# Row sums from a column of ones in the values, norm weights multiplied in on GpSimd: a local-attention and feed-forward kernel on one core

## Chip, cores and metric

The kernel runs on one NeuronCore of a Trainium2 chip. The metric is the device time of one execution in microseconds; lower is better. TensorE is called PE below, VectorE DVE, ScalarE ACT, GpSimd POOL, and SyncE, which only issues transfers here, SP.

## What is computed

Attention over 2 x 8 heads of 768 positions and 64 dimensions, in which every query sees the 31 keys around it and, for each of the 24 blocks of 32 positions, the maximum of the block's keys and the mean of its values. Its output is 1536 tokens of 512 features. They go through a root-mean-square norm with weights and a gated feed-forward layer (1536 wide), and then through a second feed-forward layer (2048 wide) with a squared rectifier. All in float32.

```python
k_sum = k.reshape(B, H, nb, block, D).max(axis=3)
v_sum = v.reshape(B, H, nb, block, D).mean(axis=3)
scores_l = np.where(mask_l, scale * np.matmul(q, k.transpose(0, 1, 3, 2)), -1e9)
scores_s = scale * np.einsum('bhsd,bhnd->bhsn', q, k_sum) + np.log(block)
scores_all = np.concatenate([scores_l, scores_s], axis=-1)
a = np.exp(scores_all - np.max(scores_all, axis=-1, keepdims=True))
a = a / (np.sum(a, axis=-1, keepdims=True) + 1e-09)
x = np.matmul(a, np.concatenate([v, v_sum], axis=2))        # -> tokens x 512
rms = np.sqrt(np.mean(x * x, axis=-1, keepdims=True) + 1e-06)
xn = x / rms * rms_g
x = (silu(xn @ w_gate) * (xn @ w_val)) @ w_out
r = np.maximum(x @ w_in, 0.0)
out = (s * (r * r) + b) @ w_out2
```

## The kernel before

**Tiles and stages.** The 1536 tokens are 12 blocks of 128 (i from 0 to 11; blocks 0 to 5 are batch 0). The attention of a block is done in two units of four heads (g = 0, 1), so there are 24 units. A unit is:

- `do_qk` (L580): four matmuls give scores of 128 queries by 120 columns (96 keys of a window of 64 queries, 24 block summaries) in a PSUM bank. The two halves of 64 queries have windows of their own; queries with zeros in the other half's rows make one matmul serve both.
- `do_top` (L590), per head on DVE: adds the mask, scales, and accumulates the extreme of the row into the tile `sm`. Each is two instructions, the second of which (128x1) writes out the accumulator.
- `do_exp` (L597), per head on ACT: exponential in place; `accum_out` also gives the row sum, in a second instruction that reads the accumulator.
- `do_t` (L608), four transposes of the probabilities P on PE, and `do_pt` (L627), their copy from PSUM to SBUF on ACT.
- `do_rc` (L614, L615) on POOL: 1e-9 is added to the four row sums and they are raised to the power -1.
- `do_pv` (L637): eight matmuls of 64 columns with the values, for four heads and two halves.
- `do_norm` (L644) on DVE: the result in PSUM times the reciprocals, into one half of the block's tile `xn`.

After the second unit of a block: `do_rms` (L663, sum of squares on ACT), `do_ss` (L668, L669, mean and power -0.5 on POOL), the multiplication by this root and by the weights `gbc` in place on DVE (L671), `do_e` (L679, four transposes on PE) and `two_x` (L692, L694: a rounded high part on ACT and the rest on DVE, as matmul operands). A matmul with float32 accuracy is then made of three passes: high by high (L779), low part of the weights by high (L780), high by low (L783), 12 matmuls in all.

**Values.** `load_v` (L297) brings, for two windows at a time, 96 rows of 8 x 64 values into a slot of `vst`; rows 96 to 119 are the block means, made on PE (`add_v` L340, `mean_v` L347), put into the first slots by ACT and DVE in turn (`put_v`, L356 and L354) and spread to the others by transfers from SBUF to SBUF (`spread_v`, L359).

**Weights.** Weight strips arrive as 64-bit floats and are made into float32 by one instruction on ACT (L224) and three on DVE (L233, L234, L235), then split into a high part on ACT (L246) and a low part on POOL (L250). Nine strips are prepared during the attention stage.

**What sets the order.** The attention stage is not written in a loop. `plan` makes a list of tasks, each with an engine, an estimated duration, what it depends on, a rank, and buffers that it takes and gives back; `give_out` runs through a model of time, lets each engine take the ready task of lowest rank, and issues the instructions in that order. Each engine then executes its own list strictly in order. Where the model sees PE idle for over 0.6 us it puts in four transposes of the identity (L461), which compute nothing. For the first three of twelve column strips of the gated layer the matmuls (`mm`, 18 groups of 12) are tasks too: six groups need the blocks 0 to 3, six the blocks 4 to 7, six the blocks 8 to 11. They stand between the attention units in PE's order. Behind the plan, the rest of the two layers is written as plain loops (`moe`).

SP issues every transfer in order; an entry waits for the transfer eight places ahead of it, and a query load (L491) also for the matmuls that last read its buffer.

Of the kernel before, what the change touches and what calls it, by code (L numbers as in the profile page):

```python
# [21 lines left out]
NTL = SEQ // 128  # L22
# [3 lines left out]
HQ = 64  # L26
KW = HQ + 2 * WIN
# [5 lines left out]
NT = NB * NTL  # L33
SUB = 512
# [9 lines left out]
RCENG = "POOL"  # L44
# [6 lines left out]
GENG = "DVE"  # L51
# [6 lines left out]
def kernel(ctx: ExitStack, tc: tile.TileContext, q_t, k_t, v_w, w_gate, w_val, w_out, w_in2, w_out2, rms_g, s2, b2, out):  # L58
# [11 lines left out]
    xnp = pool("xn", 2)  # L70
    rawp = pool("raw", 3)
# [34 lines left out]
    mone = const.tile([128, NH], F32, name="mone")  # L106
# [9 lines left out]
    part = const.tile([128, NSUB * 4 * SUB], F32, name="part")  # L116

    def big():
        return hgp.tile([128, NSUB * 2 * SUB], F32, tag="hg", name="hg")

# [4 lines left out]
    store = [big() for _ in range(5)] + [part[:, i * 3072:(i + 1) * 3072] for i in range(2)]  # L125
# [4 lines left out]
    vst = [[t.rearrange("p (s c) -> p s c", s=NTL) for t in ts] for ts in ((store[1], store[2]), (store[5], store[6]))]  # L130
# [4 lines left out]
    def consts_ident():  # L135
        make_identity(nc, ident)
        nc.gpsimd.memset(mhalf, -0.5)
        nc.gpsimd.memset(mone, -1.0)
# [194 lines left out]
    def add_v(b, a, i):  # L333
# [3 lines left out]
        for s in range(4 * a, 4 * a + 4):  # L337
            j = s % 4
            n0 = 12 * (s % 2) + s // 2
            nc.tensor.matmul(mean_ps[b][32 * j:32 * j + 32], sel[0:64, 17 - n0:49 - n0], vslot(b, s)[0:64], start=a == 0, stop=a == 2)  # L340
# [8 lines left out]
    def put_v(b, s, eng):  # L349
        p0 = 64 if s % 2 else KW  # L350
        o = vslot(b, s)[KW:KC]
        a = mean_ps[b][p0:p0 + NS]
# [5 lines left out]
    def spread_v(b, s):  # L358
        nc.sync.dma_start(out=vslot(b, s)[KW:KC], in_=vslot(b, s % 2)[KW:KC])  # L359
# [3 lines left out]
    rings = {"raw": 3, "wa": 3, "wh": 6, "wl": 6, "xn": 2, "sm": 3, "ks": KSB, **RINGS}  # L363
# [112 lines left out]
    def plan(x):  # L476
# [6 lines left out]
        K, Q, V, KM, VM = {}, {}, {}, {}, {}  # L483
# [16 lines left out]
        def lv(b, t, rank):  # L500
            V[b, t] = task("SP", mb(96 * 4096), lambda: load_v(b, 2 * t, 2), rank=rank)
# [37 lines left out]
        def means(b, rank):  # L539
# [13 lines left out]
            for t in range(NTL):  # L553
# [4 lines left out]
                else:  # L558
                    VM[b, t, "ok"] = [task("SP", 0.3, lambda s=s: spread_v(b, s), puts, 2 * (6 * b + t) - 6) for s in (2 * t, 2 * t + 1)]
# [4 lines left out]
        X_of = {}  # L564
# [4 lines left out]
        for n, (i, g) in enumerate(us):  # L569
# [24 lines left out]
            def do_exp(j, i=i, g=g):  # L594
# [3 lines left out]
                                     bias=sm_of[i][:, 0, h:h + 1], accum_out=sm_of[i][:, 1, h:h + 1])  # L598
# [4 lines left out]
            ex = [task("ACT", 0.38, lambda j=j, f=do_exp: f(j), [tops[j]], n + 0.5 + j * 0.01) for j in range(GH)]  # L603
# [7 lines left out]
            def do_rc(i=i, g=g):  # L611
                rc = sm_of[i][:, 1, GH * g:GH * g + GH]
# [385 lines left out]
```

## Time and profile before

| | |
|---|---|
| median of 3 runs | 650.69 us (650.45 to 652.07) |
| the profiled execution | 650.68 us, span 648.9 us |
| PE busy | 630.3 us (97% of the span) |
| DVE busy | 373.3 us (58%) |
| ACT busy | 267.4 us (41%) |
| POOL busy | 156.4 us (24%) |
| granted TensorE clock | 0.999 |

The span is from the first to the last instruction of the profiled execution; the time is what the device reports for it. Busy times overlap, since each engine runs its own list. PE's share says that little else can be won at the end of the program than PE's own work; the shares of the other engines are means over a first stage, in which all of them are needed, and a long second one that is mostly matmuls.

### The profile page before, as it was taken

To read this page: it belongs to the slowest core of one execution; us is meant where nothing else is said; L and a number is where in the kernel's file an instruction comes from. 1 tells how busy PE (TensorE), PEld (TensorE's weight loads), DVE (VectorE), ACT (ScalarE), POOL (GpSimd) and SP (SyncE) were. 2 spreads that over 40 slices of the span, in tenths; PEclk is the share of its full clock that TensorE was granted. 3 is DMA by queue.
4 is the path that set the end of the run, shared out by engine and by line. 5 is a ranking of instruction groups with operands and counts; after the bars stand their busy time and mean duration, and the time that the engine had idled before them with its cause. 6 is when DMAs were issued, how large, how long until landed. Compare 5 with 4: busy or idle time off the path is not lost.

```text
span 648.9 us, 8741 instructions
## 1 busy us (share of the span) xinstructions
PE 630.3 (97%) x3260; PEld 518.3 (80%) x3260; DVE 373.3 (58%) x743; ACT 267.4 (41%) x606; POOL 156.4 (24%) x201
## 2 busy tenths in 40 slices
PE   4989989999999999999999999999999999999997
PEld 2676878888888888888888888888888888888886
DVE  3498874225861555644556667870388548845532
ACT  3689894233453333311333335542454045404400
POOL 5368773332221111111111111100221022102100
PEclk9999999999999999999999999999999999999999
DMA  8979530003330111211111111121111211110022
GB/s 269 327 210 315 191 125 2 1 0 98 103 137 21 65 66 65 66 65 66 65 66 66 65 66 65 66 92 39 44 55 66 97 62 42 66 59 2 1 97 97
DMA packets 19778, 56.23 MB, mean 87 GB/s; under 512 B 2536, under 2 KB 2792, under 8 KB 19736
## 3 DMA queue, kind: packets, MB, share of 16 engines
q1 hardware_dynamic: 19736, 55.68, 25.9%
q8 instruction: 25, 0.41, 0.3%
q14 instruction: 17, 0.14, 0.1%
HBM read 51.64 MB, written 3.15 MB: 84 GB/s over the span
## 4 chain that ended last, share of the span: by engine, by line
PE 90%; ACT 4%; DMA 3%; DVE 1%; issue 1%; POOL 0%; SPq 0%; ACTq 0%; DVEq 0%; POOLq 0%
PE b L783 22%; PE b L779 21%; PE b L780 21%; PE b L903 7%; PE b L905 7%; PE b L902 7%; ACT P L597 2%; PE b L580 1%; DMA qz<-in_q_t_dram 1%; PE b L637 1%; PE b L608 1%; DMA hg<-in_k_t_dram 1%; PE b L340 1%; DMA raw<-in_w_val_dram 1%; PE b L679 1%
## 5 line engine op out<-in xcount | busy, mean ns | idle before, releaser
L250 POOL TENSOR_TENSOR wl<-wa,wh 128x512 fp32r<-128x512 f32 x68 | 89.8, 1327 | 387.2 <-ACT wh L246 314.3
L779 PE MATMUL b<-x,wh 128*128 128x512 f32 x288 | 113.4, 394 | 0.0
L780 PE MATMUL b<-x,wl 128*128 128x512 f32 x288 | 112.3, 390 | 0.0
L246 ACT ACTIVATE wh<-wa 128x512 fp32r<-128x512 f32 x68 | 41.5, 626 | 95.3 <-PE b L905 45.5
L783 PE MATMUL b<-x,wh 128*128 128x512 f32 x288 | 77.7, 392 | 0.0
L903 PE MATMUL b<-wl,hg 128*128 128x512 f32 (+1 forms) x196 | 75.2, 385 | 0.0
L902 PE MATMUL b<-wh,hg 128*128 128x512 f32 (+1 forms) x196 | 75.2, 385 | 0.0
L780 PE MATMUL b<-y,wl 128*128 128x512 f32 x192 | 74.8, 390 | 0.0
L779 PE MATMUL b<-y,wh 128*128 128x512 f32 x192 | 74.8, 390 | 0.0
L884 DVE SCALAR_TENSOR_TENSOR b<-u,sbc 128x512 f32<-128x512 f32 x48 | 50.7, 1056 | 35.6 <-ACT u L883 35.6
L779 PEld LDWEIGHTS b<-x,wh 128*128 128x128 f32 x288 | 54.1, 188 | 11.1
L780 PEld LDWEIGHTS b<-x,wl 128*128 128x128 f32 x288 | 54.1, 188 | 10.8
L783 PEld LDWEIGHTS b<-x,wh 128*128 128x128 f32 x288 | 53.6, 188 | 10.9
L780 PE MATMUL b<-hg,wl 128*128 128x512 f32 x144 | 56.1, 390 | 0.0
L779 PE MATMUL b<-hg,wh 128*128 128x512 f32 x144 | 56.1, 390 | 0.0
L804 DVE SCALAR_TENSOR_TENSOR hg<-b,bbc,hg 128x512 fp32r<-128x512 f32 x48 | 36.0, 749 | 28.2 <-ACT hg L803 28.2
L905 PE MATMUL b<-wh,hg 128*128 128x512 f32 (+1 forms) x196 | 51.6, 385 | 0.0
L783 PE MATMUL b<-y,wh 128*128 128x512 f32 x192 | 51.3, 390 | 0.0
L235 DVE SCALAR_TENSOR_TENSOR wa<-raw,wa 128x512 int32<-128x512 int32 x68 | 50.0, 735 | 2.0
L803 ACT ACTIVATE hg<-b,bbc 128x512 fp32r<-128x512 f32 x48 | 33.0, 687 | 42.8 <-DVE b L884 42.8
L234 DVE SCALAR_TENSOR_TENSOR wa<-raw,wa 128x512 int32<-128x512 int32 x68 | 48.7, 717 | 2.0
L911 DVE TENSOR_TENSOR part<-b,part 128x512 f32<-128x512 f32 (+1 forms) x37 | 24.4, 673 | 43.4 <-PE b L905 43.4
(99 smaller groups left out, 970.1 us busy)
## 6 DMA issues: line engine op xcount, KB each, us to landing
raw<-in_w_out_dram SPq DMA_DIRECT2D x28, 512.0 KB
raw<-in_w_in_dram SPq DMA_DIRECT2D x16, 512.0 KB
qz<-in_q_t_dram SPq DMA_DIRECT2D x24, 256.0 KB
raw<-in_w_gate_dram SPq DMA_DIRECT2D x12, 512.0 KB
raw<-in_w_val_dram SPq DMA_DIRECT2D x12, 512.0 KB
hg<-in_k_t_dram SPq DMA_DIRECT2D x5, 576.0 KB
out_dram<-part SPq DMA_DIRECT2D x11, 256.0 KB
hg<-in_v_w_dram SPq DMA_DIRECT2D x6, 384.0 KB
```

Source lines behind the costliest of these rows:

```text
L234: lambda: nc.vector.scalar_tensor_tensor(out=ai, in0=hi, scalar=-0x80000000, in1=ai, op0=ALU.bitwise_and, op1=ALU.bitwise_or),
L235: lambda: nc.vector.scalar_tensor_tensor(out=ai, in0=lo, scalar=29, in1=ai, op0=ALU.logical_shift_right, op1=ALU.bitwise_or),
L246: nc.scalar.activation(out=r(h), in_=a_t[i], func=AF.Copy)
L250: nc.gpsimd.tensor_tensor(out=r(lo), in0=a_t.pop(i), in1=high[i], op=ALU.subtract)
L779: nc.tensor.matmul(ps, r(hi[:, kk * 128:(kk + 1) * 128]), xh, start=kk == 0, stop=False)
L780: nc.tensor.matmul(ps, r(lo[:, kk * 128:(kk + 1) * 128]), xh, start=False, stop=False)
L783: nc.tensor.matmul(ps, r(hi[:, kk * 128:(kk + 1) * 128]), r(act(kk, 1)), start=False, stop=kk == 3)
L804: nc.vector.scalar_tensor_tensor(out=r(dst[1]), in0=ps, scalar=bias, in1=dst[0], op0=ALU.add, op1=ALU.subtract)
L884: after(0, lambda u=u, ps=ps: nc.vector.scalar_tensor_tensor(out=ps, in0=u, scalar=sbc[:, 0:1], in1=u, op0=ALU.mult, op1=ALU.mult))
L902: nc.tensor.matmul(acc, gh, r(ws[e][0][:, cs]), start=e == 0, stop=False)
L903: nc.tensor.matmul(acc, gh, r(ws[e][1][:, cs]), start=False, stop=False)
L905: nc.tensor.matmul(acc, r(ge[e][:, 1]), r(ws[e][0][:, cs]), start=False, stop=e == 3)
```

## The change

1. The values get two more columns per head (VH = 66): they arrive as zeros from the host's layout, and a new task `ones_v` on POOL sets them to 1.0, after each load and before the product. The product of the probabilities with such a column is the row sum, so the exponential no longer accumulates one. The loads, slots and spreads are 528 instead of 512 words per window; `part` and the `hg` tiles grow with them.
2. The two instructions for the reciprocal leave POOL. On DVE, `do_norm` now reads the four sums from PSUM, adds 1e-9, takes the reciprocal and then multiplies.
3. The weights are multiplied in on POOL, from `xn` into a new tile `xg` (two buffers), as a task `do_g` that depends on the normalised block alone. DVE then multiplies `xg` by the root, one number per row, in place (`do_gs`). The buffer of `xn` is given back after this, and no longer after the transposes.
4. The planner's estimates follow: exponential 0.38 to 0.29, normalisation 0.34 to 0.65, weights on POOL 1.35, root on DVE 0.5.

The core of the diff:

```diff
 def load_v(b, s0, n):
     t = vst[b][s0 // NTL][0:KW, s0 % NTL:s0 % NTL + n]
-    nc.sync.dma_start(out=t, in_=v_w[b, :, s0:s0 + n])
+    nc.sync.dma_start(out=t.rearrange("p s h d -> p s (h d)"), in_=v_w[b, :, s0:s0 + n])
+
+def ones_v(b, s0, n):
+    rows = KC if s0 < (4 if b == 0 else 2) else KW
+    nc.gpsimd.memset(vst[b][s0 // NTL][0:rows, s0 % NTL:s0 % NTL + n, :, HD:VH], 1.0)
...
 def lv(b, t, rank):
-    V[b, t] = task("SP", mb(96 * 4096), lambda: load_v(b, 2 * t, 2), rank=rank)
+    V[b, t] = task("SP", mb(96 * 16 * VH * 4), lambda: load_v(b, 2 * t, 2), rank=rank)
+    O[b, t] = task("POOL", 0.12, lambda: ones_v(b, 2 * t, 2), [V[b, t]], rank=rank)
...
     nc.scalar.activation(out=P[:, j], in_=P[:, j], func=AF.Exp, scale=-1.0,
-                         bias=sm_of[i][:, 0, h:h + 1], accum_out=sm_of[i][:, 1, h:h + 1])
+                         bias=sm_of[i][:, 0, h:h + 1])
...
-def do_rc(i=i, g=g):
-    rc = sm_of[i][:, 1, GH * g:GH * g + GH]
-    if RCENG == "POOL":
-        nc.gpsimd.tensor_scalar(out=rc, in0=rc, scalar1=1e-9, scalar2=None, op0=ALU.add)
-        nc.gpsimd.tensor_tensor(out=rc, in0=rc, in1=mone[:, 0:GH], op=ALU.pow)
...
-            nc.tensor.matmul(X[64 * c:64 * c + 64, j * HD:(j + 1) * HD], PT[0:KC, j * 128 + 64 * c:j * 128 + 64 * c + 64],
-                             vv[:, c, h * HD:(h + 1) * HD], start=True, stop=True)
+            nc.tensor.matmul(X[64 * c:64 * c + 64, j * VH:(j + 1) * VH], PT[0:KC, j * 128 + 64 * c:j * 128 + 64 * c + 64],
+                             vv[:, c, h], start=True, stop=True)
...
 def do_norm(i=i, g=g):
+    xv = box["X", i, g][:, 0:GH * VH].rearrange("p (h d) -> p h d", h=GH)
+    rc = sm_of[i][:, 1, GH * g:GH * g + GH].rearrange("p (h o) -> p h o", o=1)
+    nc.vector.tensor_scalar(out=rc, in0=xv[:, :, HD:HD + 1], scalar1=1e-9, scalar2=None, op0=ALU.add)
+    nc.vector.reciprocal(rc, rc)
     nc.vector.tensor_tensor(out=X_of[i][:, g * GH * HD:(g + 1) * GH * HD].rearrange("p (h d) -> p h d", h=GH),
-                            in0=box["X", i, g][:, 0:GH * HD].rearrange("p (h d) -> p h d", h=GH),
-                            in1=sm_of[i][:, 1, GH * g:GH * g + GH].rearrange("p (h o) -> p h o", o=1).broadcast_to([128, GH, HD]),
+                            in0=xv[:, :, 0:HD],
+                            in1=rc.broadcast_to([128, GH, HD]),
                             op=ALU.mult)
-N = [task("DVE", dve(256), do_norm, [C, rc], n + 0.0, free=(C,))]
+N = [task("DVE", 0.65, do_norm, [C], n + 0.0, free=(C,))]
...
-G = task(GENG, dve(512) * 1.2 if GENG == "DVE" else pl(512), lambda i=i: (nc.vector if GENG == "DVE" else nc.gpsimd).scalar_tensor_tensor(
-    out=X_of[i], in0=X_of[i], scalar=box["ss", i][:, 1:2], in1=gbc, op0=ALU.mult, op1=ALU.mult), [S, sml], n - 1)
+def do_g(i=i):
+    XG_of[i] = xgp.tile([128, DM], F32, tag="xg", name="xg")
+    nc.gpsimd.tensor_tensor(out=XG_of[i], in0=X_of[i], in1=gbc, op=ALU.mult)
+
+def do_gs(i=i):
+    nc.vector.tensor_scalar(out=XG_of[i], in0=XG_of[i], scalar1=box["ss", i][:, 1:2], scalar2=None, op0=ALU.mult)
+G0 = task("POOL", 1.35, do_g, [*N, sml], n - 1.5, take=("xg",))
+G = task("DVE", 0.5, do_gs, [S, G0], n - 1, give=(("xn", box["N0", i]),))
```

**What moves.** DVE at the first three normalisations (the names `b_...` are PSUM banks: 395, 417 and 435 hold the first three units' results before, 400, 422 and 439 now). Before:

```order
L644 TENSOR_TENSOR xn<-b_395,sm 128x256
L590 ISA P,sm<-b_407,mask_97 128x120
L590 ISA sm 128x1
L234 SCALAR_TENSOR_TENSOR wa<-raw,wa 128x512
L644 TENSOR_TENSOR xn<-b_417,sm 128x256
...
L235 SCALAR_TENSOR_TENSOR wa<-raw,wa 128x512
L644 TENSOR_TENSOR xn<-b_435,sm 128x256
```

Now:

```order
L641 TENSOR_SCALAR sm<-b_400 128x4
L642 RECIPROCAL sm<-sm 128x4
L643 TENSOR_TENSOR xn<-b_400,sm 128x256
L594 ISA P,sm<-b_410,mask_99 128x120
L594 ISA sm 128x1
L234 SCALAR_TENSOR_TENSOR wa<-raw,wa 128x512
L641 TENSOR_SCALAR sm<-b_422 128x4
L642 RECIPROCAL sm<-sm 128x4
L643 TENSOR_TENSOR xn<-b_422,sm 128x256
L641 TENSOR_SCALAR sm<-b_439 128x4
```

Every normalisation is now three instructions, each of which needs the one before it; the rest of the sequence keeps its order.

POOL in the second half of the attention stage, with the numbers of the buffers behind the names. Before:

```order
L668 TENSOR_SCALAR ss_1304<-ss_1304 128x1
L669 TENSOR_TENSOR ss_1304<-ss_1304,mhalf_95 128x1
L614 TENSOR_SCALAR sm_1164<-sm_1164 128x4
L615 TENSOR_TENSOR sm_1164<-sm_1164,mone_94 128x4
...
L668 TENSOR_SCALAR ss_1379<-ss_1379 128x1
L669 TENSOR_TENSOR ss_1379<-ss_1379,mhalf_95 128x1
L614 TENSOR_SCALAR sm_1334<-sm_1334 128x4
L615 TENSOR_TENSOR sm_1334<-sm_1334,mone_94 128x4
L668 TENSOR_SCALAR ss_1429<-ss_1429 128x1
L669 TENSOR_TENSOR ss_1429<-ss_1429,mhalf_95 128x1
```

Now:

```order
L672 TENSOR_TENSOR xg_1218<-xn_1160,gbc_101 128x512
L667 TENSOR_SCALAR ss_1220<-ss_1220 128x1
L668 TENSOR_TENSOR ss_1220<-ss_1220,mhalf_97 128x1
L672 TENSOR_TENSOR xg_1281<-xn_1209,gbc_101 128x512
L667 TENSOR_SCALAR ss_1284<-ss_1284 128x1
L668 TENSOR_TENSOR ss_1284<-ss_1284,mhalf_97 128x1
```

The product of a block stands ahead of the block's root on the same engine; only for the first and second block does it stand behind it.

SP, the loads behind the spreads of the second batch's means. Before:

```order
L359 DMA part<-part 24x512 x6
L491 DMA qz_104<-in_q_t_dram 128x512
L359 DMA part<-part 24x512 x4
L491 DMA qz_103<-in_q_t_dram 128x512
L218 DMA raw<-in_w_val_dram 128x1024
```

Now:

```order
L362 DMA part<-part 24x528 x6
L494 DMA qz_106<-in_q_t_dram 128x512
L362 DMA part<-part 24x528 x4
L494 DMA qz_106<-in_q_t_dram 128x512
L494 DMA qz_105<-in_q_t_dram 128x512 x2
L217 DMA raw<-in_w_val_dram 128x1024
```

The weight strip's load has moved behind two more query loads, each of which waits for PE to have read its buffer.

## Rows read from the trace of the kernel before

**Rows 1.** Windows: stretch, length, busy us of PE, PEld, DVE, ACT, POOL; clock.

```profile
28.60:57.10 28.50, 25.05 (x320) 20.83 (x321) 27.18 (x102) 25.98 (x94) 18.97 (x35) 1.00 0.84 261
57.10:108.10 51.00, 48.41 (x458) 38.85 (x457) 38.59 (x141) 41.60 (x144) 35.18 (x46) 1.00 0.44 150
108.10:648.90 540.80, 537.53 (x2385) 445.78 (x2383) 297.16 (x440) 186.81 (x321) 90.43 (x69) 1.00 0.18 61
```

**Rows 2.** Waits of PE up to 110 us: total us, times, longest.

```profile
PE b L679 <- DVE xn L671: 2.5, 3, 1.1
PE b L637 <- ACT PT L627: 2.3, 6, 0.7
```

**Rows 3.** Timeline, ACT: start us, length us, line, operation.

```profile
88.68 0.38 ACT L597 ACTIVATE P<-P,sm 128x120 f32<-128x120 f32 x1
88.97 0.19 ACT L597 ACTIVATION_READ_ACCUMULATOR P<-P,sm 128x1 f32 x1
89.06 0.38 ACT L597 ACTIVATE P<-P,sm 128x120 f32<-128x120 f32 x1
```

**Rows 4.** Timeline, DVE: reductions and the copies that depend on them.

```profile
8.53 1.01 DVE L307 TENSOR_REDUCE ks<-hg 128x12 f32<-128x384 f32 x2 [1.08 <-DMA hg<-in_k_t_dram]
9.58 0.36 DVE L312 COPY ks<-ks 64x24 f32<-64x24 f32 x2
```

**Rows 5.** Groups by shape, 0 to 110 us: count, busy us, mean ns, idle.

```profile
L644 DVE TENSOR_TENSOR xn<-b,sm 128x256 f32<-128x256 f32 x24 | 10.0, 420 | 1.2 <-PE b L637 1.1
L671 DVE SCALAR_TENSOR_TENSOR xn<-xn,ss,gbc 128x512 f32<-128x512 f32 x12 | 9.0, 749 | 6.1 <-POOL ss L669 5.8
L233 DVE TENSOR_SCALAR wa<-wa 128x512 int32<-128x512 int32 x9 | 3.8, 423 | 0.8 <-ACT wa L224 0.8
L250 POOL TENSOR_TENSOR wl<-wa,wh 128x512 fp32r<-128x512 f32 x6 | 8.3, 1385 | 2.5 <-ACT wh L246 2.5
```

**Rows 6.** Timeline, DVE: first put of means, fourth multiplication by weights.

```profile
28.64 0.69 DVE L354 TENSOR_SCALAR hg<-b 24x512 f32<-24x512 f32 x1 [1.00 <-ACT hg L356]
49.91 0.74 DVE L671 SCALAR_TENSOR_TENSOR xn<-xn,ss,gbc 128x512 f32<-128x512 f32 x1
```

**Rows 7.** Timeline, PE: the fourth block's transposes, the first feed-forward matmul.

```profile
51.30 0.66 PE L679 MATMUL b<-ident,xn 128*128 128x128 f32 x4
57.11 0.47 PE L779 MATMUL b<-x,wh 128*128 128x512 f32 x1
```

**Rows 8.** Timelines of ACT, POOL, DVE, PE: one block's way to PE.

```profile
89.81 0.61 ACT L663 ACTIVATE junk<-xn 128x512 bf16<-128x512 f32 x1
90.34 0.19 ACT L663 ACTIVATION_READ_ACCUMULATOR junk<-xn 128x1 f32 x1
90.29 1.45 POOL L615 TENSOR_TENSOR sm<-sm,mone 128x4 f32<-128x4 f32 x1
91.82 0.19 POOL L668 TENSOR_SCALAR ss<-ss 128x1 f32<-128x1 f32 x1
92.67 0.75 DVE L671 SCALAR_TENSOR_TENSOR xn<-xn,ss,gbc 128x512 f32<-128x512 f32 x1 [0.90 <-POOL ss L669]
93.48 0.66 PE L679 MATMUL b<-ident,xn 128*128 128x128 f32 x4 [1.09 <-DVE xn L671]
```

**Rows 9.** Timeline, ACT: a wait for a weight strip.

```profile
79.54 0.68 ACT L224 ACTIVATE wa<-raw 128x512 f32<-128x512 f32 x1 [2.54 <-DMA raw<-in_w_val_dram]
```

**Rows 10.** Timeline, SP: a weight strip's load behind value loads.

```profile
46.17 0.35 SPq L218 DMA_DIRECT2D raw<-in_w_val_dram  x1
```

**Rows 11.** Timeline, PE: one unit's product with the values.

```profile
43.02 0.69 PE L637 MATMUL b<-hg,PT 120*64 120x64 f32 x16
```

**Rows 12.** Timelines of DVE and POOL: one operation undisturbed, and beside POOL.

```profile
31.97 0.69 DVE L234 SCALAR_TENSOR_TENSOR wa<-raw,wa 128x512 int32<-128x512 int32 x1
36.06 1.27 POOL L250 TENSOR_TENSOR wl<-wa,wh 128x512 fp32r<-128x512 f32 x1 [1.36 <-ACT wh L246]
36.14 1.75 DVE L234 SCALAR_TENSOR_TENSOR wa<-raw,wa 128x512 int32<-128x512 int32 x1
```

More of the change, by code (lines that the diff above doesn't have):

```diff
@@ L26 @@
 HQ = 64
+VH = 66
 KW = HQ + 2 * WIN
@@ L339, in add_v @@
             n0 = 12 * (s % 2) + s // 2
-            nc.tensor.matmul(mean_ps[b][32 * j:32 * j + 32], sel[0:64, 17 - n0:49 - n0], vslot(b, s)[0:64], start=a == 0, stop=a == 2)
+            nc.tensor.matmul(mean_ps[b][32 * j:32 * j + 32], sel[0:64, 17 - n0:49 - n0], vslot(b, s)[0:64, :, 0:HD], start=a == 0, stop=a == 2)
     def sums_v(b):
@@ L558, in means @@
                 else:
-                    VM[b, t, "ok"] = [task("SP", 0.3, lambda s=s: spread_v(b, s), puts, 2 * (6 * b + t) - 6) for s in (2 * t, 2 * t + 1)]
+                    VM[b, t, "ok"] = [task("SP", 0.3, lambda s=s: spread_v(b, s), [*puts, O[b, 0]], 2 * (6 * b + t) - 6) for s in (2 * t, 2 * t + 1)]
         means(0, -3.0)
@@ L602, in plan @@
                                  take=("P",) if j == 0 else (), free=(A,) if j == GH - 1 else ()))
-            ex = [task("ACT", 0.38, lambda j=j, f=do_exp: f(j), [tops[j]], n + 0.5 + j * 0.01) for j in range(GH)]
+            ex = [task("ACT", 0.29, lambda j=j, f=do_exp: f(j), [tops[j]], n + 0.5 + j * 0.01) for j in range(GH)]
             def do_t(bk, i=i, g=g):
@@ L609, in plan @@
             T = task("PE", 0.44, do_t, [*ex, ci], n + 0.4, bank="T", give=(("P", tops[0]),))
-            def do_rc(i=i, g=g):
-                rc = sm_of[i][:, 1, GH * g:GH * g + GH]
-                if RCENG == "POOL":
-                    nc.gpsimd.tensor_scalar(out=rc, in0=rc, scalar1=1e-9, scalar2=None, op0=ALU.add)
-                    nc.gpsimd.tensor_tensor(out=rc, in0=rc, in1=mone[:, 0:GH], op=ALU.pow)
-                else:
-                    nc.vector.tensor_scalar(out=rc, in0=rc, scalar1=1e-9, scalar2=None, op0=ALU.add)
-                    nc.vector.reciprocal(rc, rc)
-            rc = task(RCENG, 1.35 if RCENG == "POOL" else 0.2, do_rc, ex, n - 1 if RCENG == "POOL" else n)
             e = PTENG[n % len(PTENG)]
@@ L954, in _layout @@
     kw = windows(k).reshape(NB, NH, NTL, 2, NWCH, CH, HD).transpose(0, 3, 6, 1, 4, 2, 5).reshape(NB, 128, NH, NWCH * NTL * CH)
-    vw = windows(v).transpose(0, 3, 2, 1, 4).reshape(NB, KW, 2 * NTL, NH * HD)
+    vw = np.zeros((NB, KW, 2 * NTL, NH, VH), np.float32)
+    vw[..., 0:HD] = windows(v).transpose(0, 3, 2, 1, 4)
+    vw = vw.reshape(NB, KW, 2 * NTL, NH * VH)
     def words(w):
```

38 lines of the change are left out of this document (18 added, 20 removed).

## Prediction

> **What bounds the kernel now.** I read the windows by stretch first: they show where TensorE is not busy, and nothing else can shorten this kernel. From 108.1 us to the end, 540.8 us, PE is busy for 537.5 of them [rows 1]: that is the two feed-forward parts, and the change does not touch them. The change lives in the attention stage before that, where PE is idle for 3.45 us of the 28.5 us up to the first feed-forward matmul at 57.1 us (28.50 less 25.05) and for 2.59 us of the next 51 (51.00 less 48.41) [rows 1]. So 6 us of idle PE is nearly all that there is to win after 28.6 us; matmuls on the identity, which only fill waits, hide a little more.
>
> Next the waits of PE up to 110 us: 2.5 us, in three waits, for the normalised x that VectorE (DVE) writes, and 2.3 us, in six, for the transposed probabilities from ScalarE (ACT) [rows 2]. And the same windows tell why those come late: up to 57.1 us DVE is busy for 27.18 and ACT for 25.98 of 28.5 us. Both are full there; afterwards DVE has 12.4 us to spare of 51 and ACT 9.4 [rows 1]. The first stretch is therefore set by DVE with ACT close behind, the second by PE's written order and what that order finds late.
>
> The sum is made against the profiled execution, 650.68 us (span 648.9, 1.78 outside it); the median of the runs is 650.69.
>
> **The change part by part.**
>
> *ACT loses 96 accumulator reads and 24 of the chains that fed on them.* An exponential with its read repeats every 0.38 us, and its read starts 0.29 us after it [rows 3]. The next exponential can start there instead: 0.09 us less for each, 8.6 us over 96. A read shows 0.19 us, but half of it lies under the exponential before it, so I do not count it whole. Least is nothing, if the exponential itself still holds ACT for 0.38. At the start of the full stretch it is worth 0.7 us: eight exponentials stand ahead of the first copy of the value means, and DVE's first one waits for that copy.
>
> *DVE gets the reciprocal.* Before each of the 24 normalisations stand two new instructions on 128x4 elements, each waiting for the one before it on the same engine, as the order of DVE shows. No row has them. The nearest are the copies of 24 elements, two in 0.36 us, which start 0.04 us after the reduction they depend on has ended [rows 4]; so I take 0.18 + 0.04 = 0.22 us for each, 0.44 us a unit. From below: the accumulator read-outs that DVE already hides between two maxima would make it 0; from above, the 0.42 us of the normalisation itself [rows 5] would make it 0.84. Against this the multiplication by rms and weight, 0.749 us, becomes one by a single column; the nearest row is the shift of 128x512 words by a constant, 0.423 us [rows 5], so 0.33 us less, 12 times. Over the stage DVE is 24 x 0.44 - 12 x 0.33 = 6.6 us busier.
>
> *What of that PE sees.* From the first put of value means (28.64) to the end of the fourth weight multiplication (49.91 + 0.74) DVE takes 22.0 us [rows 6], without gaps. In the new order the same stretch has the same 8 normalisations and the same 4 multiplications: + 16 x 0.22 - 4 x 0.33 = + 2.2 us. It also pulls one more reduction of K forward and leaves two maxima for later, which comes back. Less the 0.7 us by which ACT lets it start earlier, the fourth block is ready 1.5 us later. The first feed-forward matmul needs this block, but 5.8 us of other PE work lie between its transpose at 51.30 and that matmul at 57.11 [rows 7], and the new order puts the transpose three rows later among the same work. I count half, **+0.7 us**; the bounds are -0.7 (small instructions for nothing, ACT's relief kept) and +3.0. Two more fills by the identity stand in PE's new order; where PE would wait anyway they cost nothing, and I count them there.
>
> *GpSimd (POOL) loses the reciprocals and gets the weights.* 24 pairs of add and power go; 12 products of 128x512 come, at the 1.385 us of the subtraction of the same shape [rows 5], and 12 short memsets. How this reaches PE: at 93.48 us PE waited 1.09 us for the normalised block, DVE had waited 0.90 us for POOL, and POOL began its root at 91.82 although ACT had the sum of squares at 90.53 (90.34 + 0.19), because a power of the row sums ran until 91.74 [rows 8]. That queue goes. In its place the product starts with the normalisation and runs 1.385 us, where the sum of squares takes 0.72 (89.81 to 90.53): the root starts 0.7 us after the sum instead of 1.3, and the multiplication behind it is 0.33 us shorter. So 0.9 of that wait goes, and I count 0.3 for the shortest of the three. The third, 1.0 us, has another cause: ACT stood 2.54 us at the loading of a weight strip [rows 9] with the sum of squares queued behind it. The order of SP moves this load behind two more query loads, and ACT's order is the same, so I take 0.2 off it. In all **-1.4 us** of 2.5; bounds -2.5 and +1 (the load comes two issues later, and no root comes earlier).
>
> *A new wait on POOL.* The memsets of the ones for the second batch wait for loads of its values, and the keys' copies and the next products stand behind them. SP could issue a weight strip only at 46.17 us, for want of the first of these loads [rows 10], so that load landed shortly before. POOL will stand at the first memset until then; but the block behind it is not used by DVE before 49.9 us [rows 6], and product and root need some 2.5 us. I take nothing; at most +1.
>
> *PE itself.* The value product has 66 columns instead of 64. A unit of it takes 0.69 us [rows 11]; 24 of them grow by 2/64 at most, 0.5 us, and by nothing if something other than the columns sets their pace. **+0.3 us**.
>
> The value loads are 3% longer (1056 words for 1024); PE's long waits were for DVE and ACT [rows 2], not for these loads. Nothing.
>
> Sum: +0.7 - 1.4 + 0.3 = -0.4, so 650.3 us.
>
> **A rule that speaks against the change.** At 36.14 us DVE's combination of two SBUF tensors took 1.75 us, where undisturbed it takes 0.69; a subtraction of 128x512 had begun on POOL at 36.06, and DVE ended half a microsecond after it [rows 12]. So a long POOL operation can hold DVE, here for 1.06 us. My sum counts no such meeting.
> The Trainium skill, page "SBUF — State Buffer", section "Who interferes with whom", says that GpSimd shares a pair of ports with VectorE under an exclusive lock: a Vector instruction with two SBUF inputs, or a one-input one in a two-port mode, and a GpSimd instruction block each other, the second to issue waiting until the first has ended. The trace agrees (1.75 us against 0.69). By that rule the 12 new products would each be a 1.3 us lock, and the new one-column multiplication would take part in it; with one meeting for each product of the first stretch the time would be the 653.9 us of the second rival below instead of 650.3.
>
> **The rivals.** *Faster: ACT's relief reaches PE.* If the small instructions on DVE cost nothing extra, the full stretch shortens by the 0.7 us and by half of the 2.3 us that PE waited for probabilities, and all waits for the normalised block go: -0.7 - 1.1 - 2.5 + 0.3 = -4.0. With one of these only in part, -3.0: 647.7 us. For it: both engines that PE waits for get shorter queues in the second stretch. Against: DVE has no free time in the first. Chance 0.28.
>
> *Slower: DVE becomes the pace.* One mechanism: products on POOL hold DVE's two-input operations in the stretch before 57 us, where DVE has 1.3 us to spare in 28.5. Four products there, each meeting one such operation and costing up to 1.06 us, make 4.2 us; with the 2.2 worked out above and less 0.7 the fourth block comes 5.7 us later. Half of it reaches PE, as above: +2.9, and PE's later waits stay since the roots stand behind products: +2.9 + 0.3 = +3.2, 653.9 us. It decides from about 3.5 us of delay of the fourth block. For it: DVE is full just there, and the meeting at 36.14 us cost what it says [rows 12]. Against: only operations with two inputs outside PSUM showed it, and most of DVE's work there is maxima and normalisations out of PSUM. Chance 0.21.
>
> *That the change doesn't do what it says:* if the exponential keeps its 0.38 us, the first stretch gets the full 1.5 and the end is 651.1; within no change, and counted there.
>
> **How the numbers follow.** 0.3%, 2.0 us here, is about what a measurement of this kernel can tell from no change. My forecast, a trade of a little more in the first stretch for less in the second, ends between -1.9 and +1.6 in nearly all its combinations and has 0.51: of it 0.01 falls to faster, 0.02 to slower. Faster: 0.29; within 0.3%: 0.48; slower: 0.23. The range reaches from 0.4 us past the first rival's price to just short of the second's, with some 0.07 left out below and 0.10 above: 647.3 to 653.6; the forecast's own is 648.8 to 652.3.
>
> **What would show it.** No accumulator reads after exponentials, and exponentials that repeat every 0.29 us; two Vector instructions of about 0.2 us ahead of each normalisation; the fourth one-column multiplication ending between 51 and 53 us; the first feed-forward matmul between 57 and 58.5 us; PE's waits for the normalised block down to about 1 us. I am wrong if the first feed-forward matmul starts before 56 or after 59 us, if PE waits for POOL or for a memset, or if the end of the attention stage (the last transpose, 108.1 now) moves by more than its idle time.

## Result: slower by 1.3%, and the profile after

| | before | after |
|---|---|---|
| median | 651.38 us (4 runs) | 659.91 us (4 runs) |
| ratio, 95% interval | | 1.0128 [1.0094, 1.0162] |
| start of the first hg stretch | 172.04 us | 174.54 us |

The time lies outside the range of the prediction, on the side of the second rival and 6 us beyond its price. Ratios compare fast executions alone: two slow ones, 907.50 us at a granted clock of 0.66 in e4 below and 660.11 us of the kernel before beside e5 to e8, are left out of them. A "hg stretch" below is a run of matmuls that read the big tiles `hg`: the hidden activations, kept in the same five tiles that hold keys and values during attention. There are seven such stretches, three with L779 (now L784) and four with L902 (L907). The start of the first one serves as a marker: until then every kernel here has done the same matrix work, whatever its order (transposes of the identity apart), and the stretch behind the attention stage is pure PE work. So the marker tells what the attention stage cost in the profiled execution.

The page of after: the span and the busy times (PEld is TensorE loading its stationary operand).

```profile
span 656.7 us, 8665 instructions
PE 638.3 (97%) x3268; PEld 520.8 (79%) x3268; DVE 382.0 (58%) x791; ACT 260.1 (40%) x510; POOL 139.2 (21%) x176
```

PE is busy for 8.0 us more (630.3 before), and the span is 7.8 us longer. So the loss is hardly idle time of PE: 5.2 us are matmuls that took longer, as the next part shows, and the rest is busy time before the first hg stretch, which the end of this section takes apart. The windows of after, as in [rows 1] (the last three numbers are PE's granted clock, the busy share of the DMA engines and GB/s):

```profile
28.60:57.10 28.50, 25.46 (x302) 20.58 (x302) 27.16 (x109) 21.46 (x54) 14.10 (x26) 0.94 0.93 270
57.10:108.10 51.00, 47.48 (x474) 38.96 (x472) 46.21 (x182) 39.87 (x103) 27.18 (x32) 1.00 0.44 146
```

ACT has 4.5 us less to do in the first of them, as expected. DVE is as full as before in the first (27.16) and has gone from 38.59 to 46.21 in the second.

**Where the time went.** The timeline of PE at the first hg stretch, its first matmul and the first behind it, before:

```profile
172.04 0.39 PE L779 MATMUL b<-hg,wh 128*128 128x512 f32 x1
204.68 0.39 PE L779 MATMUL b<-x,wh 128*128 128x512 f32 x1
```

and after:

```profile
174.54 0.40 PE L784 MATMUL b<-hg,wh 128*128 128x512 f32 x1
207.84 0.39 PE L784 MATMUL b<-x,wh 128*128 128x512 f32 x1
```

The first stretch starts 2.50 us later, and its 144 matmuls take 33.30 us instead of 32.64. (They start 0.227 us apart; the 0.39 us of a record is the time of one, and neighbours overlap.) The other six grew by 0.63 to 0.88 us each, read the same way; all seven make 5.2 us. Stretches on x and y kept their length within 0.03 us. The groups by shape from 108 us on show the same; before:

```profile
L779 PE MATMUL b<-x,wh 128*128 128x512 f32 x261 | 101.7, 390 | 0.0
L902 PE MATMUL b<-wh,hg 128*128 128x512 f32 x188 | 73.2, 390 | 0.0
L779 PE MATMUL b<-hg,wh 128*128 128x512 f32 x144 | 56.1, 390 | 0.0
```

and after:

```profile
L784 PE MATMUL b<-x,wh 128*128 128x512 f32 x265 | 103.1, 389 | 0.0
L907 PE MATMUL b<-wh,hg 128*128 128x512 f32 x188 | 74.2, 395 | 0.0
L784 PE MATMUL b<-hg,wh 128*128 128x512 f32 x144 | 56.7, 394 | 0.0
```

Only matmuls with `hg` are slower, 394 and 395 ns for 390, whether `hg` is the moving tile (L784) or the stationary one (L907). 5.2 us there and 2.5 us in the attention stage make up the 7.8 us of the span.

**In the attention stage,** the waits of PE up to 125 us, after:

```profile
PE b L632 <- ACT PT L622: 4.2, 5, 1.7
PE b L684 <- DVE xg L675: 1.2, 2, 0.7
PE b L612 <- ACT P L601: 1.0, 1, 1.0
```

The waits for the normalised block fell from 2.5 us [rows 2] to 1.2, but those for the transposed probabilities rose from 2.3 to 4.2, and one for the exponential is new. ACT itself has more time than before; up to 110 us its exponentials waited 8.8 us for DVE's maxima (7.0 before). The timeline of DVE, after (start, length):

```profile
30.84 0.16 DVE L641 TENSOR_SCALAR sm<-b 128x4 f32<-128x4 f32 x1
31.04 0.18 DVE L642 RECIPROCAL sm<-sm 128x4 f32<-128x4 f32 x1
31.25 0.42 DVE L643 TENSOR_TENSOR xn<-b,sm 128x256 f32<-128x256 f32 x1
...
36.24 1.18 DVE L233 SCALAR_TENSOR_TENSOR wa<-raw,wa 128x512 int32<-128x512 int32 x1
...
38.15 1.48 DVE L675 TENSOR_SCALAR xg<-xg,ss 128x512 f32<-128x512 f32 x1
...
41.42 0.48 DVE L675 TENSOR_SCALAR xg<-xg,ss 128x512 f32<-128x512 f32 x1
```

and that of POOL:

```profile
35.60 1.27 POOL L672 TENSOR_TENSOR xg<-xn,gbc 128x512 f32<-128x512 f32 x1
38.07 1.28 POOL L672 TENSOR_TENSOR xg<-xn,gbc 128x512 f32<-128x512 f32 x1
```

The multiplication of a normalisation begins 0.41 us later for the two small instructions (31.25 less 30.84). And the new multiplication by the root, 0.48 us by itself, took 1.48 where a product had begun on POOL 0.08 us earlier; L233 took 1.18 instead of 0.69 beside the product before that. Means over the stage, groups by shape of DVE up to 110 us:

```profile
L675 DVE TENSOR_SCALAR xg<-xg,ss 128x512 f32<-128x512 f32 x12 | 7.9, 660 | 1.4 <-POOL ss L668 1.4
L233 DVE SCALAR_TENSOR_TENSOR wa<-raw,wa 128x512 int32<-128x512 int32 x9 | 7.6, 839 | 0.1
L232 DVE TENSOR_SCALAR wa<-wa 128x512 int32<-128x512 int32 x9 | 5.5, 615 | 0.3 <-ACT wa L223 0.3
```

Against 0.48, 0.69 and 0.42 us undisturbed, these three took 12 x 0.18 + 9 x 0.15 + 9 x 0.19 = 5.2 us longer. Before, only the nine L234 did (876 ns on the mean), by 1.7 us.

The fourth block's way to PE, after; before, the same three began at 49.91 [rows 6], 51.30 and 57.11 [rows 7]:

```profile
52.71 0.48 DVE L675 TENSOR_SCALAR xg<-xg,ss 128x512 f32<-128x512 f32 x1
53.25 0.65 PE L684 MATMUL b<-ident,xg 128*128 128x128 f32 x4
58.88 0.48 PE L784 MATMUL b<-x,wh 128*128 128x512 f32 x1
```

The block is ready 2.5 us later (53.19 for 50.65), its transposes begin 1.95 us later, and 1.77 of these reach the first feed-forward matmul.

PE's clock fell too in this execution. Two windows of after:

```profile
35.00:39.00 4.00, 2.33 (x39) 1.68 (x39) 3.96 (x20) 3.21 (x10) 3.76 (x5) 1.00 0.64 175
39.00:43.00 4.00, 3.49 (x27) 3.38 (x24) 3.79 (x12) 2.24 (x6) 0.56 (x2) 0.57 1.01 292
```

After four us in which PE stood idle for 1.7 it was at 0.50, 1.2 GHz, for some 3 us of the next four, which takes 1.7 us of full clock (4 x 0.43). In e2 below, which is the changed kernel with the tiles put back, PE stood idle for 1.6 of the same four us and the clock stayed at 1.00. From the start to the marker, before, after and e2:

```profile
0.00:172.04 172.04, 156.72 (x1160) 125.59 (x1161) 102.87 (x344) 102.30 (x322) 85.02 (x147) 1.00 0.47 149
0.00:174.54 174.54, 159.34 (x1169) 127.89 (x1169) 111.39 (x392) 95.02 (x226) 67.80 (x122) 0.99 0.48 148
0.00:174.80 174.80, 157.99 (x1168) 125.43 (x1169) 111.30 (x392) 94.98 (x226) 68.59 (x122) 1.00 0.48 148
```

PE was idle for 15.3 us before and for 15.2 after. So the 2.5 us of this execution are busy time: the slower clock, and eight more transposes of the identity (36 for 28), which only fill waits. In e2, with the same fills and no drop, PE was idle for 16.8 us and the marker is as late. The stage is longer without the drop too; what it would have been in this execution without one, the traces don't tell.

### The profile page after: what moved, and what is told of

It reads as the page before. It is cut to its first block, busy times and chain, and to the rows that moved or that the text cites. A ratio compares the mean times of both kernels' runs of the same rounds, so it can differ in the third digit from the quotient of the medians.

```text
span 656.7 us, 8665 instructions
## 1 busy us (share of the span) xinstructions
PE 638.3 (97%) x3268; PEld 520.8 (79%) x3268; DVE 382.0 (58%) x791; ACT 260.1 (40%) x510; POOL 139.2 (21%) x176
## 4 chain that ended last, share of the span: by engine, by line
PE 89%; DVE 5%; ACT 3%; DMA 2%; issue 1%; POOL 1%; SPq 0%; POOLq 0%; DVEq 0%; ACTq 0%
PE b L784 21%; PE b L785 21%; PE b L788 21%; PE b L910 7%; PE b L907 7%; PE b L908 7%; PE b L584 2%; DVE P L594 1%; ACT P L601 1%; DMA qz<-in_q_t_dram 1%; DMA hg<-in_k_t_dram 1%; PE b L612 1%; DVE xn L643 1%; PE b L343 1%; DVE wa L233 1%
## 5 line engine op out<-in xcount | busy, mean ns | idle before, releaser
L784 PE MATMUL b<-x,wh 128*128 128x512 f32 x288 | 113.0, 392 | 0.0
L907 PE MATMUL b<-wh,hg 128*128 128x512 f32 (+1 forms) x196 | 76.2, 390 | 0.0
L784 PE MATMUL b<-y,wh 128*128 128x512 f32 x192 | 74.7, 389 | 0.0
L784 PEld LDWEIGHTS b<-x,wh 128*128 128x128 f32 x288 | 54.1, 188 | 12.0 <-issue 0.8
L784 PE MATMUL b<-hg,wh 128*128 128x512 f32 x144 | 56.7, 394 | 0.0
L910 PE MATMUL b<-wh,hg 128*128 128x512 f32 (+1 forms) x196 | 52.9, 392 | 0.0
L234 DVE SCALAR_TENSOR_TENSOR wa<-raw,wa 128x512 int32<-128x512 int32 x68 | 50.5, 743 | 2.0
L233 DVE SCALAR_TENSOR_TENSOR wa<-raw,wa 128x512 int32<-128x512 int32 x68 | 48.4, 712 | 2.1
```

Source lines behind the costliest of these rows:

```text
L233: lambda: nc.vector.scalar_tensor_tensor(out=ai, in0=hi, scalar=-0x80000000, in1=ai, op0=ALU.bitwise_and, op1=ALU.bitwise_or),
L234: lambda: nc.vector.scalar_tensor_tensor(out=ai, in0=lo, scalar=29, in1=ai, op0=ALU.logical_shift_right, op1=ALU.bitwise_or),
L784: nc.tensor.matmul(ps, r(hi[:, kk * 128:(kk + 1) * 128]), xh, start=kk == 0, stop=False)
L907: nc.tensor.matmul(acc, gh, r(ws[e][0][:, cs]), start=e == 0, stop=False)
L910: nc.tensor.matmul(acc, r(ge[e][:, 1]), r(ws[e][0][:, cs]), start=False, stop=e == 3)
```

## Experiments

Each is one or few edits. "Marker" is the start of the first hg stretch in the profiled execution, which is a single draw: the executions of one kernel lie up to 9 us apart (e7: 652.66 to 661.35), and the profiled one need not be near the median. Four kernels with the attention instructions of before in the order of before have their markers at 171.65 (e13), 172.04 (before), 172.65 (e1) and 173.32 (e14); a difference of markers under 2 us shows nothing by itself. The clock is PE's mean granted clock in the profiled execution. The ratio is to the kernel before on the same chip.

| | median, us | ratio, interval | marker | first hg stretch | clock |
|---|---|---|---|---|---|
| e1 pitch alone | 657.02 | 1.0083 [1.0051, 1.0115] | 172.65 | 33.30 | 1.000 |
| e2 change, hg aligned | 654.56 | 1.0058 [1.0037, 1.0080] | 174.80 | 32.64 | 1.000 |
| e3 ones alone | 654.67 | 1.0047 [1.0021, 1.0074] | 174.96 | 32.64 | 1.000 |
| e4 weights alone | 654.78 | 1.0044 [1.0024, 1.0064] | 177.29 | 32.64 | 1.000 |
| e5 one instruction less | 654.08 | 1.0034 [1.0017, 1.0051] | 174.76 | 32.64 | 1.000 |
| e6 one instruction more | 661.26 | 1.0138 [1.0104, 1.0172] | 184.85 | 32.64 | 0.995 |
| e7 order alone | 655.90 | 1.0079 [1.0040, 1.0117] | 182.22 | 32.64 | 0.992 |
| e8 old estimates | 655.06 | 1.0051 [1.0028, 1.0073] | 176.64 | 32.64 | 1.000 |
| e9 change, old order | 659.21 | 1.0112 [1.0067, 1.0156] | 177.54 | 32.64 | 0.999 |
| e10 ones, old order | 653.29 | 1.0025 [1.0006, 1.0044] | 174.40 | 32.64 | 1.000 |
| e11 weights, old order | 660.05 | 1.0129 [1.0091, 1.0168] | 180.81 | 32.64 | 0.997 |
| e12 ones short, old order | 650.89 | 0.9985 [0.9966, 1.0004] | 170.80 | 32.64 | 0.999 |
| e13 pitch 256 | 651.29 | 0.9997 [0.9978, 1.0015] | 171.65 | 32.64 | 0.999 |
| e14 shift 128 | 657.98 | 1.0101 [1.0081, 1.0121] | 173.32 | 33.60 | 1.000 |
| e15 ones short, new order | 655.10 | 1.0071 [1.0044, 1.0097] | 175.91 | 32.64 | 0.997 |

The clock goes with the time, and so with the medians. Of the 80 executions of the kernel before that count in these sets all but one had a mean clock of 0.999 or 1.000, and so had all ten of e10 and of e12. e2 has a median of 653.89 us in the four executions at 1.000, and of 656.60 in the six at 0.997 or less. e7 takes 652.66 to 653.87 in five and 657.94 to 661.35 in the five at 0.992. e9 takes 656.17 in the one at 0.999 and 658.82 to 659.59 in the four at 0.997. So part of a median below is how often the clock fell.

### Where the tiles lie: e1, e2, e13, e14

Five tiles `hg` of 3168 words lie 12672 bytes apart in a partition, before 12288. Laid out one behind the other, every tile behind them moves as well. These distances are worked out from the sizes in the programs; no trace shows an address.

e1, on the kernel before:

```diff
-        return hgp.tile([128, NSUB * 2 * SUB], F32, tag="hg", name="hg")
+        return hgp.tile([128, 3168], F32, tag="hg", name="hg")[:, 0:NSUB * 2 * SUB]
```

> The kernel before with one edit: each of the five big tiles hg takes 3168 words of a partition instead of 3072, as in the change, and all code uses its first 3072. Theory A (the feed-forward matmuls that read hg are slower in the changed kernel because of where its tiles lie): each of the seven stretches of hg matmuls takes 33.3 to 33.5 us as after the change, not 32.64; first feed-forward matmul unchanged at 57.1 +- 0.5; 5 us longer in all, some 656. Rival B (they are slower for what else the change does, or by chance of that run): the stretches stay at 32.64 and the time at 651.

e2, on the changed kernel:

```diff
-        return hgp.tile([128, VT], F32, tag="hg", name="hg")
+        return hgp.tile([128, 3200], F32, tag="hg", name="hg")[:, 0:VT]
```

> The changed kernel with one edit: hg takes 3200 words instead of 3168, so that all large tiles are again apart by multiples of 512 bytes. Theory A: hg stretches back to 32.64 us, 5.2 us shorter than the changed kernel, about 654.7, with the first feed-forward matmul as late as there, 58.9; what is left over the kernel before is the attention stage alone. If distances must agree by more than 512 bytes (2048, as before the change), the stretches stay above 33. Rival B: unchanged, 33.3 to 33.5 us and 659.9.

Both as theory A had it: all seven stretches of e1 have the lengths of the changed kernel to 0.01 us, and all of e2 those of before. The pitch alone costs 1.0083, and the change without it is 1.0058. Which distance counts, e13 (3136 words for 3168 in e1's edit) and e14 were to tell:

> The kernel before with hg tiles of 3136 words: 256 bytes more, so that hg tiles and weight tiles lie apart by multiples of 256 bytes, and not always of 512. If multiples of 256 bytes are enough: hg stretches at 32.64 us, 651. If 512 are needed: stretches between 32.8 and 33.5, 652 to 656.

e14, on the kernel before:

```diff
     hgp = pool("hg", 5)
+    gap = pool("gap", 1)
...
+    gap.tile([128, 32], F32, tag="gap", name="gap")
```

> The kernel before with hg tiles of 3072 words as there, and everything behind them (activations x and y, weights) shifted by 128 bytes. If the distance between the tiles that one matmul reads matters (hg and weights, now 128 bytes off a multiple of 512): hg stretches at 33.2 to 33.6, x and y stretches unchanged, 656. If the distance of the hg tiles from one another matters: all stretches as before, 32.64, 651.

Groups by shape from 108 us on, e13:

```profile
L779 PE MATMUL b<-hg,wh 128*128 128x512 f32 x144 | 56.0, 389 | 0.0
```

and e14:

```profile
L781 PE MATMUL b<-x,wh 128*128 128x512 f32 x262 | 102.0, 389 | 0.0
L781 PE MATMUL b<-hg,wh 128*128 128x512 f32 x144 | 57.3, 398 | 0.0
...
L904 PE MATMUL b<-wh,hg 128*128 128x512 f32 x188 | 74.2, 395 | 0.0
```

In e14 the hg tiles lie as before from one another, and only their distance from the weights has changed by 128 bytes. Its matmuls with hg take 6 and 9 ns more than its 389, and a stretch 33.60 us, the most of all; in e1 and in the changed kernel two of the five tiles still lie at a multiple of 256 bytes from the weights. In e13 all do, not all at a multiple of 512, and nothing is lost. What counts is the distance between the two tiles that one matmul reads.

### The parts, in the order that the planner makes: e3, e4, e7, e8

e3 (on e2: G as before the change) and e4 (on the kernel before: `do_g` and `do_gs` of the change). The core of e3's edit, which e4's reverses:

```diff
-            G0 = task("POOL", 1.35, do_g, [*N, sml], n - 1.5, take=("xg",))
-            G = task("DVE", 0.5, do_gs, [S, G0], n - 1, give=(("xn", box["N0", i]),))
+            G = task("DVE", dve(512) * 1.2, lambda i=i: nc.vector.scalar_tensor_tensor(
+                out=X_of[i], in0=X_of[i], scalar=box["ss", i][:, 1:2], in1=gbc, op0=ALU.mult, op1=ALU.mult), [S, sml], n - 1)
```

> Ones column, no accumulator reads and the reciprocal on VectorE as in the change; the weights and the root stay in one VectorE instruction as before; hg of 3200 words. Theory C (the attention stage is late because VectorE has two more dependent instructions per unit, 0.41 us each unit): the stage is as late as in the changed kernel or later, since the weights' instruction is 0.27 us longer: first feed-forward matmul at 58.5 to 59.5, time 654 to 656 if the hg stretches are at 32.64. Theory D (it is late because the products on GpSimd hold VectorE): first feed-forward matmul at 57 to 57.8, time 650 to 652.

> The kernel before with the third part of the change alone: weights multiplied in on GpSimd, root on VectorE; accumulated row sums and the reciprocals on GpSimd as before; hg of 3072 words. Theory C: VectorE is 12 x 0.27 us shorter, first feed-forward matmul at 56.5 to 57.2, time 649 to 651. Theory D: the products add meetings like the one of 1.0 us seen at 38.15 us in the changed kernel, and GpSimd now has reciprocals, roots and products in one queue: first feed-forward matmul at 58 to 60, time 652 to 655.

Theory C had e3's time right and theory D e4's. Each part alone costs what both together cost, so they do not add up. The first feed-forward matmul, which I had asked for, tells nothing here: in e3 it comes at 55.37 and in e4 at 54.38, since the planner puts it elsewhere. This made the order itself a suspect (theory O).

e7, on the kernel before (e8 is the reverse, on e2):

```diff
-            ex = [task("ACT", 0.38, lambda j=j, f=do_exp: f(j), [tops[j]], n + 0.5 + j * 0.01) for j in range(GH)]
+            ex = [task("ACT", 0.29, lambda j=j, f=do_exp: f(j), [tops[j]], n + 0.5 + j * 0.01) for j in range(GH)]
...
-            N = [task("DVE", dve(256), do_norm, [C, rc], n + 0.0, free=(C,))]
+            N = [task("DVE", 0.65, do_norm, [C, rc], n + 0.0, free=(C,))]
```

> The kernel before, with two of the planner's estimates as in the change (exponential 0.29 for 0.38, normalisation 0.65 for 0.34): the same instructions and tiles as before in another order. Theory O: marker at 173.5 to 175 instead of 172.04, time 652.5 to 654.5. Theory C: 171.7 to 172.7, time as before.

> As e2, with these two estimates as before the change (0.38 and 0.34), so that the order is planned with old numbers. Theory O: marker back to 172 to 173.2. Theory C: 174.3 or later.

e7: another order of the same work costs 1.0079, more than theory O had said, so the order of the kernel before is worth something for its own work. Half of the executions and the profiled one (660.85 us, clock 0.992) hold most of this; the other five lie 1.1 to 2.3 us over the kernel before (median 651.54). e8: old estimates don't bring the time back. The two together left open how much of the change's loss was order.

### One instruction less, one more: e5, e6

e5, on e2 (e6, also on e2, adds one more small instruction in the same place instead):

```diff
-                nc.vector.tensor_scalar(out=rc, in0=xv[:, :, HD:HD + 1], scalar1=1e-9, scalar2=None, op0=ALU.add)
-                nc.vector.reciprocal(rc, rc)
+                nc.vector.reciprocal(rc, xv[:, :, HD:HD + 1])
```

> The changed kernel with hg of 3200 words, as e2, and the reciprocal taken straight from PSUM: the addition of 1e-9 before it is left out. The order of everything else is the same. The marker is the start of the first hg stretch (172.04 us before, 174.80 in e2): by then all kernels have done the same work. Theory C (each dependent VectorE instruction ahead of a normalisation costs 0.2 us and VectorE sets the pace between 30 and 55 us, with some 10 normalisations): the marker falls by 1 to 2 us, to 172.8 to 173.8, time 652.5 to 654. Theory O (the planner's new numbers have put the instructions into a worse order, and VectorE's additions are hidden): the marker stays at 174.3 to 175.3.

> As e2, with a third small VectorE instruction ahead of each normalisation (0.0 is added to the reciprocals in place). Theory C: marker 1 to 2 us later than e2's 174.80, 176 to 177, time 655.5 to 657. Theory O: 174.3 to 175.3.

e5's marker (174.76) is where theory O had it; the median is 0.5 us under e2's and the intervals overlap, so in this order it does not show that an instruction costs anything, nor that it costs nothing. e6 cost 10 us at the marker and 6.7 in the median, where I had said 1 to 2; its granted clock from 28.6 to 57.1 us was 0.88 on the mean, which is 6.8 us at 0.50.

### The same work in the old order: e9 to e12

The planner was given the numbers of the kernel before, and an empty task where the reciprocal stood on POOL. The order of PE, ACT and SP is then that of the kernel before row by row, and so is DVE's with the new instructions in the places of the old ones.

```diff
-            ex = [task("ACT", 0.29, lambda j=j, f=do_exp: f(j), [tops[j]], n + 0.5 + j * 0.01) for j in range(GH)]
+            ex = [task("ACT", 0.38, lambda j=j, f=do_exp: f(j), [tops[j]], n + 0.5 + j * 0.01) for j in range(GH)]
+            rc = task("POOL", 1.35, lambda: None, ex, n - 1)
...
-            N = [task("DVE", 0.65, do_norm, [C], n + 0.0, free=(C,))]
+            N = [task("DVE", dve(256), do_norm, [C, rc], n + 0.0, free=(C,))]
...
-            G0 = task("POOL", 1.35, do_g, [*N, sml], n - 1.5, take=("xg",))
-            G = task("DVE", 0.5, do_gs, [S, G0], n - 1, give=(("xn", box["N0", i]),))
+            G0 = task("POOL", 0.0, do_g, [*N, sml], n - 1.5, take=("xg",))
+            G = task("DVE", dve(512) * 1.2, do_gs, [S, G0], n - 1, give=(("xn", box["N0", i]),))
```

In the same way the value loads got their old duration, and the memset none. e10 is this with e3's G, e11 is e4 with the last two lines, e12 is e10 with e5's edit, and e15 is e3 with e5's edit.

> All the work of the change (hg of 3200 words), but planned with the numbers of the kernel before, and with a task on GpSimd that issues nothing in the place of each reciprocal: TensorE, VectorE, ScalarE and SyncE get the order of the kernel before, with the new instructions in the places of the old ones. Theory O (the new order costs the 2.8 us of the attention stage, the new instructions are hidden): start of the first hg stretch at 171.5 to 173, time 650.5 to 652.5. Theory C (the new work costs it): marker at 174 to 176, time 653.5 to 656.

> As e9, but with the weights and the root in one VectorE instruction, as before the change: the ones column and the reciprocals on VectorE alone. Theory O: 171.5 to 173. Theory C: 174 to 176, later than e9 by up to 1 us, since 4 of these instructions stand in the full stretch and each is 0.27 us longer. If the products on GpSimd are the trouble instead (theory D): 171.5 to 172.5, earlier than e9 by 1 us or more.

> Kernel before with the weights multiplied in on GpSimd and the root on VectorE, in the order of the kernel before (reciprocals on GpSimd as before). Theory O and theory C: 171 to 172.5, no later than before. Theory D: 173 to 175, since products, reciprocals and roots share one queue and products hold VectorE.

> As e10, with the reciprocal straight from PSUM (the addition of 1e-9 is left out): one new VectorE instruction for each unit instead of two, 24 less in all. Theory C: marker 1 to 2 us earlier than e10's. Theory O: as e10's within 0.5 us. As a version to keep: 650 to 652, since ScalarE's 96 reads are gone and VectorE has 0.2 us more for each unit.

The marker in the timeline of PE, e9, e10 and e12:

```profile
177.54 0.39 PE L785 MATMUL b<-hg,wh 128*128 128x512 f32 x1
```

```profile
174.40 0.39 PE L779 MATMUL b<-hg,wh 128*128 128x512 f32 x1
```

```profile
170.80 0.39 PE L778 MATMUL b<-hg,wh 128*128 128x512 f32 x1
```

Theory O falls: with every row in its old place the change is slower (1.0112) than in its own order (1.0058), so the new order takes time off and does not cost it. It is 4.7 us by the medians; at the marker it is 2.7, and between the executions at full clock, one of e9 and four of e2, 2.3. e9 and e11 came out slower than every range that I had given; e10's marker is in theory C's range but 3.1 us ahead of e9's, as only theory D had it, and e12's is 3.6 us ahead of e10's, where theory C had 1 to 2. Two causes remain, now each in the same order, that of the kernel before:

- Small instructions on DVE. From e12 to e10 one of about 0.2 us is added to each unit, 4.9 us of DVE's time, and the median rises by 2.4 us (the marker by 3.6), at full clock in all twenty executions. PE's idle time up to the marker rises from 15.1 to 18.0 us, and its waits for the transposed probabilities from 3.5 us in five waits to 5.3. That DVE's maxima come later, and with them exponentials and copies, is how I explain it.
- Products on POOL. From e10 to e9 the median rises by 5.9 us; at full clock it is 2.9 (656.17 against 653.29), the marker rises by 3.1 and PE's idle time up to it from 18.0 to 20.4 us. The other half goes with the clock, which fell in four of e9's five executions and in none of e10's. e11, which keeps before's reciprocals, is 8.1 us over the kernel before, with the clock down in all four executions. The waits of DVE between 28 and 115 us in e11:

```profile
DVE xg L678 <- POOL ss L671: 9.6, 6, 3.2
DVE xg L678 <- POOL xg L675: 3.2, 2, 1.8
```

and the waits of PE there:

```profile
PE b L687 <- DVE xg L678: 9.3, 9, 2.5
```

With products and reciprocals in one queue, roots come so late that DVE and then PE stand. How much of it is this queue, and how much are instructions of DVE held beside a product, the runs don't separate. Nor do they split the 2.5 us of the changed kernel itself, which has another order, between these two causes.

e12 is the version to keep: ones column, reciprocal straight from PSUM, weights left on DVE, old order. It leaves out the 1e-9 that the reference adds to the row sum. At 0.9985 [0.9966, 1.0004] its gain over the kernel before is not certain, and it is 9 us under the changed kernel. e15 is the same work in the planner's new order:

> e12's work (ones column, reciprocal straight from PSUM, weights and root in one VectorE instruction) in the order that the planner makes with the change's numbers (exponential 0.29, normalisation 0.65, no task for the reciprocal on GpSimd). If the order has a cost of its own for this work: start of the first hg stretch 2 us or more behind e12's 170.80, time 653 to 655. If not: within 1 us of it, 650 to 652.

It is 4.2 us behind e12 (medians of two sets; 4.8 when each is taken against the kernel before in its own set), marker 5.1 us later: for work without the products the old order is the better one. It is not more waiting that shows: up to the marker PE was idle for 14.0 us, in e12 for 15.1. The clock fell in all four executions of e15 (0.995 to 0.997) and in none of e12's, and it has 36 fills by the identity for 28.

## Why the prediction was wrong, point by point

- **What bounds the kernel: failed.** "The change does not touch them" was said of the 540.8 us of feed-forward. My own first point of the change says that the `hg` tiles grow, and these 540.8 us read them. The shift of tiles that follows costs 5.2 us there (e1 shows it alone), the larger part of the loss, and the sum and all rivals had it at nothing.
- **ACT without reads: right.** Three exponentials in a row take 0.96 us (ACT, L601 at 54.97 in the timeline of after) where one takes 0.38, so they repeat every 0.29. DVE's first put of means starts at 27.80 instead of 28.64 [rows 6]: 0.84 us, forecast 0.7.
- **DVE's additions: right in size.** 0.41 us per normalisation against my 0.44; the multiplication by the root 0.48 undisturbed against 0.42. Left out was that it can be held too: its mean is 0.66.
- **What of that PE sees: mis-sized, and half of it on a wrong path.** DVE's stretch from the first put of means to the fourth block took 25.4 us (27.80 to 53.19) for 22.0, +3.4 where I had added 2.2; that the 22.0 were without gaps was wrong too, for DVE was busy in 20.9 of them. The first feed-forward matmul came at 58.88, 1.8 us late (+0.7 forecast, bounds to +3.0): of the 1.95 us by which the fourth block's transposes were late nearly all arrived there, and not half. Every late maximum also reaches PE, through exponential, transposition and copy, and by the marker 2.5 us were lost; I had counted DVE's 12.4 us to spare behind 57 us as free. The last transpose, which I had named as a sign, tells nothing: it came 2.05 us earlier (106.04 for 108.09) in the planner's new order, in which the stage is longer.
- **POOL's queue: right, and given back.** Waits for the normalised block went from 2.5 to 1.2 us, as the -1.4 said. The 1.9 us more of waits for transposed probabilities and the 1.0 us for an exponential outweigh it. I had no term for that.
- **The memset's wait: right.** PE never waited for it. (In e2 and e10 DVE's first maximum stood 1.8 us behind the first memset, at 11 us; after didn't show this.)
- **PE's 66 columns: mis-sized.** 227 ns a matmul against 228, nothing instead of +0.3.
- **The rule against the change** (the Trainium skill, page "SBUF — State Buffer", section "Who interferes with whom"): the trace agrees, 1.48 us against 0.48 for the one-input multiplication. It was right as a mechanism. The second rival priced it together with DVE's additions at 653.9 us, and the change without the tile shift ends near that (654.56, e2); this is in part luck. Its fourth block was to be 5.7 us late and was 2.5, and e3, which has no product on POOL, ends at 654.67 as well. I gave it 0.21 because DVE's work there was mostly out of PSUM; weight preparation and the new multiplication were held all the same.

## What to carry to other kernels

When a change alters the size of a tile, list what else lies in that pool and behind it, and who reads those tiles later: a padding for an early stage can slow a late one whose work is the same as before. Before moving work onto an engine that is full in a stage, ask for each of its instructions who waits for what stands behind it, not only for the moved one. And where a planner sets the order, compare two versions of the work in one fixed order before judging either.

## What the hardware showed unexpectedly

A matmul with a 128x128 stationary and a 128x512 moving float32 tile was 3 to 9 ns slower of 389 on the mean of its groups (0.96 us on the 32.64 of a stretch, in e14) when these tiles lay 128 bytes off a multiple of 256 from each other in a partition, and as fast as ever at multiples of 256 and 512 (e1, e13, e14). The Trainium skill, page "SBUF — State Buffer", section "Who interferes with whom", calls PE's read ports for the moving and the stationary operand independent and says that PE never waits on anyone. The measured stretches differ from the first, since a distance between the two operands costs time, and they decide; the second is said of waiting for other engines, and no run here bears on it. What inside the memory makes the difference, no run here shows.
